# One attention-and-experts kernel on Trainium2: one SBUF tile for all buffers, or a tile for each

## The chip, the cores and the metric

The kernel runs on one core of one Trainium2 chip. The metric is the device time of one execution in microseconds (us); the medians below are over several executions. The engines are TensorE (PE; its weight loads are listed as PEld), VectorE (DVE), ScalarE (ACT), GpSimd (POOL) and SyncE (SP), which here only issues transfers. Each engine runs its own list of instructions in order, and waits on semaphores for the others.

## The reference

Sparse attention over 8 batches, 8 heads, 576 positions and 64 features, then a mixture of 8 experts that takes at most 80 tokens each:

```python
scores = scale * np.matmul(q, k.transpose(0, 1, 3, 2))
mask_local = (rel >= 0) & (rel < stride)                       # stride 32, heads 0-3
mask_strided = (rel >= 0) & (pos[None, :] % stride == pos[:, None] % stride)   # heads 4-7
attn = softmax(np.where(masks, scores, -1e9))
x = (attn @ v)  ->  [4608, 512]
logits = x @ w_gate; expert_idx = argmax(logits)
for e in range(8):                # at most `capacity` tokens, those with the highest gates
    h = np.maximum(x[tok_idx] @ w1[e], 0.0)
    out[tok_idx] = gate_w[tok_idx, None] * (h @ w2[e])         # all other rows stay zero
```

## The kernel before

The **attention stage** works through eight batches in a software pipeline. For each batch SyncE loads `ql` and `kl` (the local heads), `qs` and `ks` (the strided heads) and the values `vl`, `va`, `vb`; q and k have two sets of buffers, which batches take in turn, and the values have one. TensorE computes the scores (L324 local, L399 strided, after mask matmuls as L320), ScalarE and VectorE the softmax (L337 to L358 local, L409 to L425 strided), VectorE transposes the weights in blocks of 32, GpSimd and ScalarE put these blocks where the second product wants them (the `c4` copies, L206 on ScalarE, L208 on GpSimd and VectorE), TensorE multiplies by the values (L378 local, L440 strided) and turns the results (L532, L537), and the rows of x go to DRAM (`xs`) through the buffers `xn` and `xr`. Gate logits are computed on the way.

The **expert stage** ranks the gates, gathers 80 rows for each expert, and multiplies by `w1` (L793) and `w2` (L821). The weights are 64 pieces of 0.52 MB, each loaded to one of 35 places in turn (`w0` to `w63`, L580) and most of them split by ScalarE and VectorE (steps `wh`, `wo`) into two half-precision pieces (L609, L611). Ten places are memory of their own; 13 lie over the q and k buffers, eight over the value and weight buffers of attention and four over `xn` and `xr`, and are taken once attention is done with these. The rows of `out` that no expert writes are filled by 18 transfers of zeros (`z0` to `z17`, L558), and the scatters (L852) write the experts' rows after them.

The **order** of the work is written out: a string `ORDER` names each step (`lk` loads kl, `sk` ks, `sq` qs, `va` and `vb` the strided values, `c4` the copies, `u` and `d` the expert products), and each engine gets its steps in that order. SyncE's list is thus fixed, with attention loads, weights, stores and zeros in one row. Waits are not written out. The tile framework derives them from the tiles and the pieces of tiles that an instruction reads and writes.

All buffers are pieces of one tile `mem` of 128 partitions by 50304 words; a class `Area` hands out column ranges. Four kinds of loads write every second or every 16th partition of their piece: `tkl[h][u::2, u, ...]` (kl, L304, and L929 ahead of the loop), `tks[h][x::2, x]` (ks, L310 and L932), `tvs[0::2]` (va, L314) and `tvs[1::16]` (vb, L315). There are 16 + 16 + 8 + 8 = 48 such transfers in the program.

Of the kernel before, what the change touches and what calls it, by code (L numbers as in the profile page):

```python
# [86 lines left out]
def moe_attention(ctx: ExitStack, tc, ql, kl, qs, ks, vl, va, vb, wg, w1, w2, cap, out):  # L87
# [60 lines left out]
    a = Area(QK)
    tql, tkl, tqs, tks = [], [], [], []
    for i in range(2):  # L150
        tql.append(a([2, S]))
        tkl.append(a([2, 2, 32 + S]))
        tqs.append(a([4, 16, 18]))
        tks.append(a([2, 4, 16, 18]))
    assert a.at == PV
    tvl, ptb, tvs, pts4 = a([2, 9, D]), a([9, 2, 160]), a([32, D]), a([32, 4, 18])
    assert a.at == CB
    pl, ptl = a([2, 9, 64]), a([2, 9, 2, 32])
    pstr = [a([32, 18]) for _ in range(2)]
    psn, pts = a([32, 32]), a([32, 32])  # L160
    assert a.at == XT
    xtl = [a([2, S]) for _ in range(2)]
    xts = [a([4, S // 2]) for _ in range(2)]
    assert a.at == ROW
    xn = [a([2, DM]) for _ in range(3)]
    xr = a([2, DM])
    assert a.at == MISC
    lt, zt = a([S // 2]), a([1024])
    small = [[a([32]) for _ in range(4)] for _ in range(2)]
    gsm = [a([18, E], parts=NQ) for _ in range(2)]  # L170
    gs1 = [a([18], parts=NQ) for _ in range(3)]
    lgs = a([48, E], parts=NQ)
    assert a.at <= SPARE
    spare = [mem[:, SPARE + 512 * i:SPARE + 512 * i + 512] for i in range(2)]
# [3 lines left out]
    a = Area(CB)  # L178
    rtb = Area(a.at)
    a.at += 1380  # L180
# [1 line left out]
    hes = [a([2, 8, SLOTS], F16) for _ in range(2)]
# [1 line left out]
    assert a.at <= XT
    a = Area(XT)
# [1 line left out]
    assert a.at <= ROW
# [376 lines left out]
    def raw(i):  # L564
        return mem[:, bases[i % NSLOT]:bases[i % NSLOT] + CH]

    def hi(i):
# [3 lines left out]
        at = bases[split[s - 2] % NSLOT]  # L571
        return mem[:, at + 512:at + CH].bitcast(F16)
# [458 lines left out]
sl1.2 vb.1 es0.0/A c4l3.0/G sq.4 sml.1 c4s1.1/A c4s3.1/G w2 lk1.3 pvl0.0/0 c4s2.1/A lk0.3 sal.1/V wh0 pvl2.0/2 srl.1
lq.3 mx1.2 nl1.1 wgl0 pvl1.0/1 el0.0/A mxs.2 lk0.4 el2.0/A nl0.1 sbs.2 rs0.0/0 el1.0/A lv.1 rs1.0/2 c4s0.1/A lk1.4
ws0.0/V rl2.0/1 sk0.4 exs.2 trl.1 ss0.3 w3 ws1.0/A sk1.4 pvs1.1/0 wl2.0/A sb1.2 c4l5.1/G pvs2.1/2 es1.1/A c4l7.1/G
sms.2 pvs0.1/1 wh1 tk mx0.2 ss1.3 es0.1/A sb0.2 c4l3.1/G rl0.0/0 es2.1/A tk1/1 c4l6.1/G ex0.2 rs0.1/2 rc1 wo0 ex1.2
ss2.3 ws0.1/A sl0.3 sml.2 c4l4.1/G c4l1.1/A sas.2/G c4l2.1/G wl0.0/A ss3.3 sal.2/V c4l0.1/A srl.2 srs.2 rl1.0/2 nl1.2
# [90 lines left out]
```

## Time and profile before

| | |
|---|---|
| time, three runs | 442.89, 443.5, 445.39 us (median 443.5) |
| the profiled execution's own time | 439.65 us |
| its span in the trace | 437.9 us, 10778 instructions |
| mean granted TensorE clock | 0.767 of full speed |
| PE / PEld / DVE / ACT / POOL busy | 245.8 / 201.8 / 198.4 / 169.4 / 106.1 us |
| busy shares | 56% / 46% / 45% / 39% / 24% |
| DMA | 84.14 MB, mean 192 GB/s |
| chain that ended last | DMA 45%, PE 19%, issue 16%, POOL 7%, DVE 6% |

The profile was taken from one execution. "Busy" is the time in which an engine carried out an instruction; the chain is followed back from the last instruction to what released each step. [...] Attention takes the span up to about 333 us, the experts the rest; the two stages have different limits, so the shares over the whole span describe neither.

### The profile page before, as it was taken

To read this page: it belongs to the slowest core of one execution; us is meant where nothing else is said; L and a number is where in the kernel's file an instruction comes from. 1 tells how busy PE (TensorE), PEld (TensorE's weight loads), DVE (VectorE), ACT (ScalarE), POOL (GpSimd) and SP (SyncE) were. 2 spreads that over 40 slices of the span, in tenths; PEclk is the share of its full clock that TensorE was granted. 3 is DMA by queue.
4 is the path that set the end of the run, shared out by engine and by line. 5 is a ranking of instruction groups with operands and counts; after the bars stand their busy time and mean duration, and the time that the engine had idled before them with its cause. 6 is when DMAs were issued, how large, how long until landed. Compare 5 with 4: busy or idle time off the path is not lost.

```text
span 437.9 us, 10778 instructions
## 1 busy us (share of the span) xinstructions
PE 245.8 (56%) x4628; PEld 201.8 (46%) x4628; DVE 198.4 (45%) x326; ACT 169.4 (39%) x265; POOL 106.1 (24%) x158
## 2 busy tenths in 40 slices
PE   2426153414805446064706438657586798879894
PEld 2314042303703345044505325536475787779872
DVE  2312543101614244061233136625397759878871
ACT  3302141201703423132223234445366348778770
POOL 4300341110800323060213123336402420111101
PEclk9955685655776679557576659888698899998998
DMA  4444632443137265323314445775398999999701
GB/s 138 159 135 163 220 147 79 158 139 103 62 108 270 80 217 153 121 82 114 111 54 172 146 158 153 296 262 190 146 381 306 374 305 411 414 395 409 302 18 34
DMA packets 24613, 84.14 MB, mean 192 GB/s; under 512 B 4273, under 2 KB 4273, under 8 KB 23986
## 3 DMA queue, kind: packets, MB, share of 16 engines
q1 hardware_dynamic: 23538, 80.79, 52.1%
q0 software_dynamic: 1024, 2.62, 1.9%
q8 instruction: 38, 0.62, 0.6%
q14 instruction: 13, 0.11, 0.1%
HBM read 63.21 MB, written 20.19 MB: 190 GB/s over the span
## 4 chain that ended last, share of the span: by engine, by line
DMA 45%; PE 19%; issue 16%; POOL 7%; DVE 6%; SPq 3%; ACT 2%; POOLq 0%; DVEq 0%; ACTq 0%
DMA mem<-kl 10%; DMA mem<-ks 7%; DMA mem<-va 7%; DMA mem<-vb 5%; DMA mem<-w 4%; DMA mem<-ql 4%; DMA xs<-mem 3%; PE bk L532 3%; POOL mem L208 3%; PE bk L378 2%; DMA mem<-xs,mem 2%; DMA mem<-qs 2%; POOL out L852 2%; PE bk L537 2%; PE bk L793 2%
## 5 line engine op out<-in xcount | busy, mean ns | idle before, releaser
L611 DVE SCALAR_TENSOR_TENSOR mem<-mem 128x1024 f16<-128x1024 f32 x60 | 72.3, 1238 | 20.8 <-DMA mem<-kl 16.1
L206 ACT COPY mem<-bk 128x512 f32<-128x512 f32 (+4 forms) x85 | 44.3, 539 | 96.3 <-DMA mem<-ks 30.8
L208 POOL COPY mem<-mem 32x576 f32<-32x576 f32 (+1 forms) x65 | 44.8, 690 | 137.4 <-DMA mem<-ks 61.2
L609 ACT ACTIVATE mem<-mem 128x1024 f16<-128x1024 f32 x60 | 62.0, 1053 | 12.5 <-DVE mem L611 8.6
L532 PE MATMUL bk<-ident,mem 128*128 128x128 f32 (+1 forms) x96 | 20.4, 355 | 56.7 <-DMA mem<-kl 21.1
L206 ACT COPY mem<-mem 32x576 f32<-32x576 f32 (+1 forms) x31 | 20.7, 668 | 57.6 <-DMA mem<-ks 21.2
L532 PEld LDWEIGHTS bk<-ident,mem 128*128 128x128 f32 (+1 forms) x96 | 14.0, 183 | 61.0 <-issue 41.2
L324 PE MATMUL sloc<-mem 128*32 128x128 f32 x576 | 26.4, 342 | 16.5 <-DMA mem<-ks 16.5
L324 PEld LDWEIGHTS sloc<-mem 128*32 128x32 f32 x576 | 20.1, 138 | 28.7 <-issue 28.1
L793 PEld LDWEIGHTS <-mem 128*128 128x128 f16 x768 | 30.4, 100 | 5.0 <-issue 4.9
L378 PE MATMUL bk<-mem 128*64 128x160 f32 (+2 forms) x352 | 28.5, 325 | 6.9 <-ACT mem L206 5.2
L821 PE MATMUL sstr<-mem 128*128 128x80 f16 x672 | 30.8, 205 | 2.7 <-issue 2.6
L378 PEld LDWEIGHTS bk<-mem 128*64 128x64 f32 x352 | 26.3, 166 | 9.4 <-issue 4.6
L537 PE MATMUL bk<-ident,mem 128*128 128x128 f32 (+1 forms) x96 | 18.7, 333 | 20.8 <-ACT mem L206 20.8
L821 PEld LDWEIGHTS <-mem 128*128 128x128 f16 x672 | 27.7, 102 | 4.6 <-issue 4.4
L399 PEld LDWEIGHTS sstr<-mem 128*18 128x18 f32 x1024 | 15.8, 124 | 27.7 <-issue 22.7
L440 PE MATMUL bk<-mem 128*64 128x72 f32 x512 | 23.5, 260 | 7.0 <-ACT mem L206 6.8
L852 POOL DMA_INDIRECT out<-mem x8 | 8.9, 1108 | 69.6 <-ACT mem L847 34.3
L440 PEld LDWEIGHTS bk<-mem 128*64 128x64 f32 x512 | 21.8, 166 | 8.3 <-ACT mem L206 7.2
L356 POOL TENSOR_TENSOR mem<-mem 128x576 f32<-128x576 f32 x16 | 18.2, 1152 | 29.5 <-DMA mem<-kl 20.0
L200 PE MATMUL sstr<-identb 128*128 128x128 bf16 x237 | 18.7, 254 | 10.3 <-DVE mem L676 4.0
L411 DVE TENSOR_TENSOR mem<-sstr,mem 128x576 f32<-128x576 f32 x8 | 6.1, 758 | 39.5 <-DMA mem<-va 16.8
(166 smaller groups left out, 376.9 us busy)
## 6 DMA issues: line engine op xcount, KB each, us to landing
mem<-w SPq DMA_DIRECT2D x64, 512.0 KB, 9.9
out<-mem SPq DMA_DIRECT2D x18, 512.0 KB, 7.1
xs<-mem SPq DMA_DIRECT2D x16, 512.0 KB, 3.4
mem<-ql SPq DMA_DIRECT2D x8, 576.0 KB, 3.8
mem<-kl SPq DMA_DIRECT2D x16, 288.0 KB, 3.0
mem<-qs SPq DMA_DIRECT2D x8, 576.0 KB, 4.7
mem<-ks SPq DMA_DIRECT2D x16, 288.0 KB, 3.0
mem<-vl SPq DMA_DIRECT2D x8, 576.0 KB, 6.3
```

The costliest lines, as they stand in the source:

```text
L200: nc.tensor.matmul(sstr[:, 896:1024], identb, identb, start=True, stop=True)
L206: nc.scalar.copy(o, i)
L208: eng[e].tensor_copy(o, i)
L324: nc.tensor.matmul(sloc[32 * g:32 * g + 32, 128 * c:128 * c + 128], tql[h][:, hh, 32 * t:32 * t + 32], tkl[h][:, :, hh, 32 * t:32 * t + 64 ...
L378: nc.tensor.matmul(t[64 * u:64 * u + 64, n0:n0 + z - a], tvl[:, u, c], ptb[:, c, u, a:z], start=(c == 3 * k), stop=(c == 3 * k - 1), tile_ ...
L440: nc.tensor.matmul(t[64 * x:64 * x + 64, c:c + 72], tvs[:, r], pts4[:, 2 * (r % 16) + r // 16].rearrange("p h j -> p (h j)"), start=True, ...
L532: nc.tensor.transpose(t[0:n, x, c], xv[:, c, x, 128 * a:128 * a + n], ident)
L537: nc.tensor.transpose(t[0:n, g], xh[:, g, 128 * a:128 * a + n], ident)
L609: op("wh%d" % i, {"ACT": 1.05}, lambda e: nc.scalar.activation(hi(i), raw(i), AF.Copy, scale=SC), [st["w%d" % i]] + prev, filler=True)
L611: op("wo%d" % i, {"DVE": 1.24}, lambda e: nc.vector.scalar_tensor_tensor(lo(i), raw(i), SC, hi(i), op0=ALU.mult, op1=ALU.subtract), [st["w ...
L793: nc.tensor.matmul(o[:, f], w[:, n:n + P], x[:, a, c], start=(c == 0 and i == 0 and f == 0), stop=(c == 3 and i == 2), skip_group_check=True)
L821: nc.tensor.matmul(o, w[:, n:n + P], x[:, b, 2 * c + a], start=(c == 0 and a == 0 and f == 0 and i == 0), stop=(c == 3 and a == 1 and i == ...
```

## The change

Every buffer becomes a tile of its own (`buf` below), one for each set where a buffer has two. The places for weights are pieces of 1024 columns inside these tiles. A place may no longer cross from one buffer into the next, so 33 places remain: ten of their own, 12 over q and k, seven over the values and copied weights and four over `xn` and `xr`. The expert stage's smaller buffers (`xes`, `hes`, `y32`, the ranking's `rt`, the gathered rows `xg`) are cut out of tiles of attention in the same way. The number of instructions on each engine stays as it was: 5061 on TensorE, 188 on SyncE, 267 on ScalarE, 318 on VectorE and 177 on GpSimd in the built programs.

```diff
-    mem = wctx.enter_context(tc.tile_pool(name="mem", bufs=1)).tile([P, MEM], F32, name="mem")
+    mem = wctx.enter_context(tc.tile_pool(name="mem", bufs=1))
+
+    def buf(name, shape, n=1, parts=P):
+        return [mem.tile([parts] + shape, F32, name=f"{name}{i}") for i in range(n)]
...
+    tql, tkl = buf("ql", [2, S], 2), buf("kl", [2, 2, 32 + S], 2)
+    tqs, tks = buf("qs", [4, 16, 18], 2), buf("ks", [2, 4, 16, 18], 2)
+    (tvl,), (ptb,), (tvs,), (pts4,) = buf("vl", [2, 9, D]), buf("ptb", [9, 2, 160]), buf("vs", [32, D]), buf("pts4", [32, 4, 18])
...
+    def places(t, m):
+        f = flat(t) if len(t.shape) > 2 else t
+        return [f[:, CH * j:CH * j + CH] for j in range(m)]
+
+    slots = buf("slot", [CH], NFREE)
+    for i in range(2):
+        slots += places(tkl[i], 2) + places(tql[i], 1) + places(tks[i], 2) + places(tqs[i], 1)
+    slots += places(ptb, 2) + places(tvs, 2) + places(pts4, 2) + places(tvl, 1)
+    for t in (*xn, xr):
+        slots += places(t, 1)
+    NSLOT = len(slots)
...
-            t = mem[0:parts, self.at:self.at + w]
-            self.at += w
+            x = next(x for x in self.tiles if x[1] + w <= x[0].shape[1])
+            t = x[0][0:parts, x[1]:x[1] + w]
+            x[1] += w
...
-    a = Area(QK)
-    tql, tkl, tqs, tks = [], [], [], []
-    for i in range(2):
-        tql.append(a([2, S]))
-        tkl.append(a([2, 2, 32 + S]))
...
-    bases = [FREE + CH * i for i in range(NFREE)] + [QK + CH * i for i in range(13)] + \
-            [PV + CH * i for i in range(8)] + [ROW + CH * i for i in range(4)]
-    NSLOT = len(bases)
...
     def raw(i):
-        return mem[:, bases[i % NSLOT]:bases[i % NSLOT] + CH]
+        return slots[i % NSLOT]
...
         if k < 6:
             return after(6, "sl1", "ss3")
-        if k < 13:
-            return after(6, "sl1", "ss3") + after(7, "sl1", "ss3")
-        if k < 21:
+        if k < 12:
+            return after(7, "sl1", "ss3")
+        if k < 19:
             return after(7, *["pv%s%d" % (x, j) for x in "ls" for j in range(3)])
-        return [[stores[12], stores[15]], [stores[13]], [stores[14]], after(4, "st2") + after(5, "st2") + after(6, "st2") + after(7, "st2")][k - 21]
+        return [[stores[12], stores[15]], [stores[13]], [stores[14]], after(4, "st2") + after(5, "st2") + after(6, "st2") + after(7, "st2")][k - 19]
...
-    rt = rtb
+    rt = Area(pl, *pstr)
```

In `ORDER` a few loads of the first four batches move by a step or two, and of the zeros z10 to z17 stand among later weights. The loops themselves are the same.

**SyncE, batch 1 of attention.** The rows are transfers in the order in which SyncE issues them, with the semaphores that each waits for where it isn't yet sure of them: `DMAHW` with a number is one of eight that count landed transfers, the others are engines. Before:

```order
L310 DMA mem_89<-ks 64x1152 [waits DMAHW5_49,DMAHW6_49,DVE_49,DMAHW7_49,Activation_49,Pool_49]
L310 DMA mem_89<-ks 64x1152 [waits DVE_49,Activation_49]
L315 DMA mem_89<-vb 8x2048 [waits DMAHW4_49,DMAHW3_49,Pool_49]
L308 DMA mem_89<-qs 128x1152 [waits DMAHW5_49,DMAHW1_49,PE_49]
L580 DMA mem_89<-w1 128x1024
L304 DMA mem_89<-kl 64x2x576 [waits DVE_49,DMAHW6_49,Activation_49,Pool_49]
L304 DMA mem_89<-kl 64x2x576 [waits Activation_49]
L307 DMA mem_89<-ql 128x1152 [waits DMAHW2_49,DMAHW1_49,DMAHW0_49]
```

After:

```order
L299 DMA ks1_96<-ks 64x1152 [waits DMAHW3_49]
L299 DMA ks1_96<-ks 64x1152 [waits DMAHW4_49]
L304 DMA vs0_99<-vb 8x2048 [waits DMAHW5_49]
L297 DMA qs0_93<-qs 128x1152 [waits DMAHW6_49,PE_49]
L568 DMA slot2_135<-w1 128x1024 [waits DMAHW7_49]
L293 DMA kl1_92<-kl 64x2x576 [waits DMAHW0_49]
L293 DMA kl1_92<-kl 64x2x576 [waits DMAHW1_49]
L296 DMA ql1_90<-ql 128x1152 [waits DMAHW2_49]
```

The transfers and their order are the same. The loads of ks, kl and vb waited for VectorE, ScalarE or GpSimd and for several transfers; each now waits for one landed transfer.

**GpSimd, the copies of batch 0 (L208 before, L201 after).** They read the transposed weights `ptl` or `pts` and write `ptb` or `pts4`. Before:

```order
L422 TENSOR_TENSOR mem_89<-mem_89 128x512 [waits DVE_49,Pool_49]
L422 TENSOR_TENSOR mem_89<-mem_89 128x64
L208 COPY mem_89<-mem_89 32x18x32 [waits DMAHW1_49,Pool_49]
L208 COPY mem_89<-mem_89 32x18x32
L208 COPY mem_89<-mem_89 32x16x32 [waits DMAHW4_49,DMAHW3_49]
L208 COPY mem_89<-mem_89 32x18x32 [waits DMAHW5_49]
L208 COPY mem_89<-mem_89 32x32x18 [waits DVE_49,PE_49]
L356 TENSOR_TENSOR mem_89<-mem_89 128x576 [waits DMAHW0_49,DVE_49,DMAHW1_49,Activation_49,Pool_49]
L356 TENSOR_TENSOR mem_89<-mem_89 128x576 [waits DMAHW4_49]
```

After:

```order
L411 TENSOR_TENSOR psn0_103<-ps1_106,sm13_124 128x512 [waits DVE_49,Pool_49]
L411 TENSOR_TENSOR psn0_103<-ps1_106,sm13_124 128x64
L201 COPY ptb0_98<-ptl0_102 32x18x32 [waits Pool_49]
L201 COPY ptb0_98<-ptl0_102 32x18x32
L201 COPY ptb0_98<-ptl0_102 32x16x32
L201 COPY ptb0_98<-ptl0_102 32x18x32
L201 COPY pts40_100<-pts0_104 32x32x18 [waits DVE_49,PE_49]
L345 TENSOR_TENSOR pl0_101<-pl0_101,sm11_122 128x576 [waits DVE_49,Activation_49,Pool_49]
L345 TENSOR_TENSOR pl0_101<-pl0_101,sm11_122 128x576
```

The copies and the products around them waited for landed transfers; now they wait for engines alone.

**SyncE, early in the expert stage: the first pieces of weights past the last place.** Before, where the 36th piece (w35) is the row with PE in its waits:

```order
L580 DMA mem_89<-w2 128x1024 [waits DMAHW1_49]
L580 DMA mem_89<-w2 128x1024 [waits DMAHW2_49]
L580 DMA mem_89<-w2 128x1024 [waits DMAHW3_49]
L558 DMA out<-mem_89 128x1024 [waits DMAHW4_49]
L558 DMA out<-mem_89 128x1024 [waits DMAHW5_49]
L580 DMA mem_89<-w2 128x1024 [waits DMAHW6_49,PE_49]
```

After, where the 34th (w33) and 35th (w34) are the rows with PE, and two of the zeros follow:

```order
L568 DMA xr0_114<-w2 128x1024 [waits DMAHW1_49]
L568 DMA slot0_133<-w2 128x1024 [waits DMAHW2_49,PE_49]
L568 DMA slot1_134<-w2 128x1024 [waits DMAHW3_49,PE_49]
L547 DMA out<-zt0_116 128x1024 [waits DMAHW4_49]
L547 DMA out<-zt0_116 128x1024 [waits DMAHW5_49]
```

Two pieces of weights that had places of their own now go to places whose last readers are TensorE's products with the third and the fourth piece of expert 0's w1 (steps u20.0 to u31.0), and two zeros stand behind them.

## Rows read from the trace of the kernel before

**Rows 1.** Windows: us from:to, length, busy time by engine, granted clock, DMA share, GB/s.

```profile
core 0: us, PE busy (x) PEld busy (x) DVE busy (x) ACT busy (x) POOL busy (x), PEclk, DMA share, GB/s
0.00:333.00 333.00, 161.93 (x2888) 124.85 (x2889) 124.64 (x222) 102.77 (x170) 87.75 (x140) 0.71 0.47 160
333.00:438.00 105.00, 83.84 (x1740) 76.91 (x1739) 73.75 (x104) 66.67 (x96) 18.32 (x19) 0.94 0.79 295
```

**Rows 2.** Chain of waits that ended last within 0 to 333 us, by line.

```profile
by line: DMA mem<-kl 13.1%; DMA mem<-ks 9.4%; DMA mem<-va 8.8%; issue 7.3%; DMA mem<-vb 6.6%; DMA mem<-ql 5.1%; DMA xs<-mem 4.2%; PE bk L532 3.7%; POOL mem L208 3.7%; DMA mem<-w 3.5%; PE bk L378 3.2%; DMA mem<-qs 2.7%; PE bk L537 2.2%; PE s
```

**Rows 3.** Waits of engines: who <- what: us in total, times, longest us.

```profile
POOL mem L208 <- DMA mem<-ks: 61.2, 6, 16.7
ACT mem L206 <- DMA mem<-ks: 52.0, 6, 13.9
```

**Rows 4.** Timeline: start us, us, engine line op, [idle before <-releaser], batch 1.

```profile
64.39 4.31 SPq L310 DMA_DIRECT2D mem<-ks  x2
71.28 0.61 POOL L208 COPY mem<-mem 32x512 f32<-32x512 f32 x1 [6.91 <-DMA mem<-ks]
71.30 2.36 PE L324 MATMUL sloc<-mem 128*32 128x128 f32 x40 [9.19 <-DMA mem<-ks]
71.92 0.61 SPq L315 DMA_DIRECT2D mem<-vb  x1
```

**Rows 5.** The page's DMA issues: times, KB each, us from issue to landing.

```profile
mem<-kl SPq DMA_DIRECT2D x16, 288.0 KB, 3.0
```

**Rows 6.** Waits of SyncE's queue.

```profile
SPq L314 <- PE bk L440: 15.7, 3, 7.5
```

**Rows 7.** Timeline of the start, SyncE and TensorE.

```profile
4.64 1.30 SPq L929 DMA_DIRECT2D mem<-kl  x2
8.71 0.34 SPq L930 DMA_DIRECT2D mem<-qs  x1
14.34 0.68 PE L399 MATMUL sstr<-mem 128*18 128x36 f32 x32 [7.19 <-DMA mem<-ks]
```

**Rows 8.** Windows, TensorE's columns alone, of L324, L440 and L399 by pairs.

```profile
22.60:42.80 20.20, 4.81 (x84) 0.50 0.47 142
264.90:281.80 16.90, 3.44 (x112) 1.00 0.74 258
84.00:114.50 30.50, 4.64 (x64) 0.50 0.34 104
264.90:281.80 16.90, 2.37 (x64) 1.00 0.74 258
84.00:114.50 30.50, 1.37 (x64) 0.50 0.34 104
264.90:281.80 16.90, 0.92 (x64) 1.00 0.74 258
```

**Rows 9.** Windows of two dense stretches, TensorE's columns alone.

```profile
264.90:281.80 16.90, 12.66 (x311) 1.00 0.74 258
316.10:333.00 16.90, 14.17 (x189) 1.00 0.90 345
```

**Rows 10.** Window in the expert stage, all columns.

```profile
390.00:410.00 20.00, 18.00 (x423) 17.54 (x421) 15.85 (x19) 15.50 (x22) 3.03 (x2) 0.91 1.03 408
```

**Rows 11.** Timeline of SyncE's queue in the expert stage.

```profile
344.94 4.78 SPq L580 DMA_DIRECT2D mem<-w  x4
351.24 2.68 SPq L558 DMA_DIRECT2D out<-mem  x2
```

**Rows 12.** Timeline of both engines, group in 0 to 333 us, the page's group.

```profile
151.50 2.88 DVE L611 SCALAR_TENSOR_TENSOR mem<-mem 128x1024 f16<-128x1024 f32 x2
151.76 1.53 POOL L208 COPY mem<-mem 32x576 f32<-32x576 f32 x1
L611 DVE SCALAR_TENSOR_TENSOR mem<-mem 128x1024 f16<-128x1024 f32 x11 | 14.2, 1308 | 16.2 <-DMA mem<-kl 16.1
L208 POOL COPY mem<-mem 32x576 f32<-32x576 f32 (+1 forms) x65 | 44.8, 690 | 137.4 <-DMA mem<-ks 61.2
```

More of the change, by code (lines that the diff above doesn't have):

```diff
@@ L126, in moe_attention, with flat, __init__ @@
     wctx = ExitStack()
-    mem = wctx.enter_context(tc.tile_pool(name="mem", bufs=1)).tile([P, MEM], F32, name="mem")
+    mem = wctx.enter_context(tc.tile_pool(name="mem", bufs=1))
+    def buf(name, shape, n=1, parts=P):
+        return [mem.tile([parts] + shape, F32, name=f"{name}{i}") for i in range(n)]
+    def flat(t):
+        d = " ".join("abcdefg"[i] for i in range(len(t.shape) - 1))
+        return t.rearrange("p %s -> p (%s)" % (d, d))
+    tql, tkl = buf("ql", [2, S], 2), buf("kl", [2, 2, 32 + S], 2)
+    tqs, tks = buf("qs", [4, 16, 18], 2), buf("ks", [2, 4, 16, 18], 2)
+    (tvl,), (ptb,), (tvs,), (pts4,) = buf("vl", [2, 9, D]), buf("ptb", [9, 2, 160]), buf("vs", [32, D]), buf("pts4", [32, 4, 18])
+    (pl,), (ptl,), (psn,), (pts,) = buf("pl", [2, 9, 64]), buf("ptl", [2, 9, 2, 32]), buf("psn", [32, 32]), buf("pts", [32, 32])
+    pstr = buf("ps", [32, 18], 2)
+    xtl, xts = buf("xtl", [2, S], 2), buf("xts", [4, S // 2], 2)
+    xn, (xr,) = buf("xn", [2, DM], 3), buf("xr", [2, DM])
+    (lt,), (zt,) = buf("lt", [S // 2]), buf("zt", [1024])
+    small = [buf(f"sm{i}", [32], 4) for i in range(2)]
+    gsm, gs1, (lgs,) = buf("gsm", [18, E], 2, NQ), buf("gs", [18], 3, NQ), buf("lgs", [48, E], 1, NQ)
+    spare = buf("spare", [512], 2)
+    def places(t, m):
[8 more added lines that the diff above has]
+    NSLOT = len(slots)
     class Area:
-        def __init__(self, at):
-            self.at = at
+        def __init__(self, *tiles):
+            self.tiles = [[t if len(t.shape) == 2 else flat(t), 0] for t in tiles]
         def __call__(self, shape, dt=F32, parts=P):
@@ L146, in __call__ @@
             return t
[L148 to L180 removed]
+    a = Area(ptl, psn, pts)
+    hes = [a([2, 8, SLOTS], F16) for _ in range(2)]
     xes = [a([2, 4, SLOTS], F16) for _ in range(2)]
[L182 removed]
     y32 = [a([4, SLOTS]) for _ in range(2)]
[L184 to L185 removed]
+    a = Area(*xtl, *xts)
     xg = [a([DM], parts=SLOTS) for _ in range(E)]
[L187 removed]
     psum = wctx.enter_context(tc.tile_pool(name="psum", bufs=1, space=PSUM))
@@ L570, in hi @@
             return spare[s].bitcast(F16)
[L571 to L572 removed]
+        return raw(split[s - 2])[:, 512:CH].bitcast(F16)
     def lo(i):
@@ L1031 @@
[L1031 to L1035, printed above, removed]
@@ L1067 @@
-gg.7 r1 rl1.7/1 rl2.7/2 wl2.7/A r3 warm/8 r2 ws1.6/A st1.6 rs1.7/2 r4 wl1.7/A st2.7 r7 rs0.7/0 st2.6 ws1.7/A r5
-ws0.7/A st0.7 st1.7 w23 r6 w24 w25 w26 w27 wh11 warm/68 r8 z8 r13 r9 z9 wh12 z10 wo11 warm/14 r10 w28 w29 w30 r11 wh13
-r12 g0 w31 w32 wo12 w33 w34 z11 r14 g1 wh14 z12 wo13 wo14 wh15 warm/102 xt0 wo15 wh16 r15 xh0 g2 wh17 xl0 wo16 warm/21
-u00.0 xt1 u01.0 wo17 xh1 u11.0 wh18 u10.0 xl1 g3 u21.0 r16 wh19 u01.1 wo18 u20.0 u11.1 w35 wo19 wh20 u21.1 u00.1 xt2
-wo20 wh21 u30.0 u31.0 hh0.0 wo21 u10.1 xh2 w36 u20.1 wh22 w37 g4 hl0.0 z13 u30.1 xl2 w38 d00.0 wh23 wo22 xt3 z14 z15
@@ new lines @@
+pvl1.7/1 wh9 gd.6 el2.7/V rs2.6/0 el1.7/A w22 wo9 wh10 gt0.7/2 ws2.6/V rl0.7/1 wo10 lt.7 gt1.7/0 wl0.7/A rl0.6/2 ga.7
+rs2.7/1 gb.7 rl1.6/0 ge.7 wl1.6/A gc.7 wl0.6/A rs0.6/0 gd.7 ws2.7/V ws0.6/A gr.7/2 rs1.6/0 st0.6 gg.7 r1 rl1.7/1
+rl2.7/2 wl2.7/A r3 warm/8 r2 ws1.6/A st1.6 rs1.7/2 r4 wl1.7/A st2.7 r7 rs0.7/0 st2.6 ws1.7/A r5 ws0.7/A st0.7 st1.7
+w23 r6 w24 w25 w26 w27 wh11 warm/68 r8 z8 r13 r9 z9 wh12 z10 wo11 warm/14 r10 w28 r11 wh13 r12 g0 w29 wo12 w30 r14 g1
+wh14 wo13 w31 wo14 wh15 w32 warm/102 xt0 wo15 wh16 r15 xh0 g2 wh17 xl0 wo16 warm/21 u00.0 xt1 u01.0 wo17 xh1 u11.0
@@ new lines @@
+wh18 u10.0 xl1 g3 u21.0 r16 wh19 u01.1 wo18 u20.0 u11.1 w33 wo19 wh20 u21.1 u00.1 xt2 wo20 wh21 u30.0 u31.0 hh0.0 wo21
+u10.1 xh2 w34 u20.1 wh22 z11 g4 hl0.0 z12 u30.1 xl2 w35 d00.0 wh23 wo22 xt3 w36 w37 d10.0 hh1.0 u31.1 z13 hh0.1 wo23
+d01.0 wh24 w38 d11.0 g5 hl0.1 z14 wh25 u00.2 hl1.0 z15 wo24 d21.0 xh3 d20.0 z16 hh1.1 d31.0 xl3 g6 wh26 d30.0 hl1.1
+z17 u10.2 wo25 ya0/A u00.3 u01.2 w39 u20.2 wo26 wh27 u11.2 u01.3 w40 wo27 u21.2 wh28 d01.1 u31.2 w41 wo28 wh29 d00.1
+d11.1 u30.2 w42 wo29 wh30 d21.1 xt4 hh0.2 wo30 w43 yx0 wh31 u10.3 d10.1 hl0.2 w44 wh32 u11.3 wo31 u20.3 hh1.2 d20.1
```

99 lines of the change are left out of this document (45 added, 54 removed).

## The prediction

> **What bounds the kernel now.** I read the windows first, by stage [rows 1]. In the expert stage, the 105 us from 333 to 438, TensorE is busy for 83.84 us at a clock of 0.94 and the DMA engines move 295 GB/s: it is near its own limits. In attention, 0 to 333 us, nothing is: TensorE is busy for 161.93 us, VectorE 124.64, ScalarE 102.77, GpSimd 87.75, and DMA runs at 160 GB/s, where the expert stage shows stretches of 408 [rows 10]. So attention is bound by waits, and TensorE's clock is down to 0.71 meanwhile.
>
> Which waits, the chain of that stage tells [rows 2]: kl 13.1, ks 9.4, va 8.8 and vb 6.6%, together 37.9% of 333 us or 126 us, are landings of the four loads that write every second or 16th partition. Transfers of more bytes hold less of it: ql 5.1, qs 2.7, weights 3.5%. The waits by engine [rows 3] then name the oddity: the copies on GpSimd and ScalarE wait 61.2 and 52.0 us for loads of ks, six times each, up to 16.7 us. These copies read transposed softmax weights and never touch ks. The order of the built programs says the same: the strided loads wait for three compute engines, and the copies behind them for transfers.
>
> One place shows the whole pattern [rows 4]. From 64.39 SyncE holds two loads of ks. GpSimd's copy starts at 71.28, after 6.91 us idle, TensorE's scores of another buffer at 71.30 after 9.19, both released by ks; at 71.92 the load of vb closes the gate again. The cause is that a load that skips partitions is ordered against every access of its tile, and all buffers are one tile: the load waits until all engines have run dry, and all engines wait until it has landed. One landing takes 3.0 us [rows 5], so 48 loads have room for 144 us of landings, of which the chain holds 126.
>
> **The change part by part.** (1) *Tiles of their own* take these orderings away. In the built program a load waits for a transfer eight places back and for real readers of its own buffer, a copy for its producers. Real waits stay: va must wait until TensorE has read the values of the batch before (15.7 us, 3 times) [rows 6]. Instructions stay the same, so nothing is added.
>
> What is late next? Cover all with TensorE, the busiest engine. Its clock of 0.71 is a mix of 1.0 and 0.5; a share s at half gives 1 − 0.5s = 0.71, s = 0.58. If busy time is spread alike, 94 us of the 162 were done at half clock. What that costs is read from equal instructions at both levels [rows 8]: L324 takes 57.3 ns each at 0.50 and 30.7 at 1.00 (1.87), L440 72.5 and 37.0 (1.96), L399 21.4 and 14.4 (1.49); mean 1.77. At full clock the work is thus 94/1.77 + 68 = 121 us. TensorE won't be busy without a gap: in the two densest stretches of attention, both at clock 1.0, it is busy for 12.66 and 14.17 of 16.90 us [rows 9], shares of 0.75 and 0.84, mean 0.795. I take that, since those stretches have the same instructions and few strided loads in them: 121/0.795 = 152 us.
>
> Ahead of this stands the start. The first scores come at 14.34 [rows 7]; the loads of kl are issued at 4.64, after ql has landed, those of qs and ks from 8.71, after kl has. Both waits go, about 5 us by SyncE's rows, which leaves 9. Attention: 152 + 9 = **161 us instead of 333**. A second way, from the chain: 333 − 126 = 207, and less the 7.8% of ql and qs (26 us), which wait in the same row, 181 with the clock as slow as now. The faster clock explains the rest.
>
> DMA has to follow: 333 us at 160 GB/s are 53.3 MB; in 161 us that is 331 GB/s, just below the 345 of the densest stretch [rows 9], with no more than 131 us at 408 [rows 10]. So it fits, closely, and the other engines, with 125, 103 and 88 us of work, fit too.
>
> (2) *33 places instead of 35.* The pieces w33 and w34, and the zeros z11 and z12 behind them, now stand behind TensorE's products of expert 0. Before, SyncE issued pieces of weights and then zeros from 344.94 on, without waiting for TensorE, and the next zeros at 351.24 [rows 11]. A piece of 0.524 MB takes 1.28 us at 408 GB/s [rows 10], so four transfers held back cost at most 5.1 us, if the queue stays full afterwards, and nothing if it catches up. I take 0, because w33 belongs to w2 of expert 3, with the products of the experts ahead of it still to come, and keep 5.1 for the range. (3) *Zeros later, loads moved by a step*: the same bytes in another order on SyncE, hidden under TensorE; their cover is the 105 us at 295 GB/s, 31 MB that need 76 us at 408. 0.
>
> (4) *More overlap of VectorE and GpSimd* may cost. Where VectorE ran two of the weight splits (L611, 2.88 us from 151.50), one copy on GpSimd took 1.53 us in place of 0.69 on average [rows 12]. [...] By the row, 11 splits [rows 12] times 0.84 us are 9 us, if all fell on the path. They need not: GpSimd is free for 73 us of 161. I take 0 and keep 9.
>
> Sum: 161 + 105 = 266 us of span. The profiled execution took 439.65 with a span of 437.9, so 1.75 more: 267.8. The median of the runs, 443.5, is 1.0088 times that execution: **270 us**.
>
> **Its own bounds.** Below: at a busy share of 0.90, as in the expert stage (18.00 of 20 us) [rows 10], attention is 121/0.90 + 9 = 143, which gives 252; I say 250. Above: a share of 0.75 (161 us) and a quarter of the work still at half clock (0.25 × 0.77 × 161 = 31), with 9 for the start and 5 for the places, give 206 + 105 + 1.75 = 313, 315 scaled. Not all of this comes at once; without the places and with half of the clock's part it is 295. I say 305.
>
> **The rivals.** *The clock stays low.* If gaps remain often enough that it is granted 0.71 as before, 162/0.795 + 9 = 213 and the time is 322. For it: whole stretches stood at 0.50, as late as 114.5 us [rows 8]. Against: the gaps there are the removed waits. *Transfers become the bound.* At the 258 GB/s of the first dense stretch [rows 9] 53.3 MB take 207 us, and with the start the time is 326. For it: at most eight transfers are in flight, in one row, and a real wait of va holds all behind it. Against: 345 and 408 GB/s with the same queue. *VectorE and GpSimd run in turns.* 124.64 + 87.75 = 212 us [rows 1], with the start 221, time 331. Against: of 65 copies the mean is 0.69 [rows 12], so few are held. *The change does half of what it says*: enough waits remain, or copies really wait for something that lands with ks; attention (333 + 161)/2 = 247, time 357.
>
> *Slower.* If the waits for ks merely stood last beside real ones that end just as late, attention keeps its 333 us, and the loss of two places decides: 5.1 us more in the expert stage, 444.8 or 449 scaled (1.2%). It takes over only where attention gains less than 5.1 us. For it: a releaser is the last of several. Against: idle times of 6.91 and 9.19 us on two engines that end within 0.02 us of each other [rows 4], and a built order in which the copy has no other wait of that kind left.
>
> **How the numbers follow.** The forecast's case (250 to 305) has 0.80; the clock 0.05, transfers 0.04, turns 0.03, half 0.02, below 250 0.02, no change that can be told 0.02, slower 0.02. About 0.5% is what a measurement of this kernel can tell from no change. Faster is 0.80 + 0.05 + 0.04 + 0.03 + 0.02 + 0.02 = 0.96. The range is the forecast's own, which leaves out 0.20.
>
> **What would show it.** Right: no wait of a copy for kl, ks, va or vb among the first waits; attention ending near 161 us with a clock of 0.9 or more and over 300 GB/s; the first scores near 9 us; the expert stage still near 105. Wrong: the clock still near 0.7 there; SyncE's waits for real readers as the chain's largest part; copies on GpSimd of over 1 us in numbers; a gap in the weights after w32 with TensorE waiting for them.

## The result and the profile after

The changed kernel takes 277.19 us (median of four runs, 274.56 to 279.69) against 444.01 for the kernel before: a ratio of 0.6187, 95% interval 0.6154 to 0.622. The four runs lie in two pairs, near 274.7 and 279.6 us; here and below, medians are over all runs, while ratios and intervals leave out a run more than 1.5% above the fastest of the same kernel. The profiled execution took 274.93 us with a span of 273.2 us and a mean granted clock of 0.947.

Windows by stage, after, with the columns of [rows 1]. The border is put, here and in every kernel below, 1.6 us after the start of the last matmuls that turn attention's results, as 333.0 is in the kernel before.

```profile
0.00:165.80 165.80, 128.78 (x2883) 104.36 (x2889) 127.01 (x223) 100.86 (x169) 86.95 (x140) 0.95 0.89 320
165.80:273.20 107.40, 84.34 (x1740) 77.04 (x1739) 73.80 (x104) 66.78 (x96) 19.00 (x19) 0.94 0.79 289
12.10:165.80 153.70, 125.64 (x2858) 101.75 (x2864) 117.78 (x210) 93.37 (x162) 78.56 (x116) 0.94 0.90 325
```

Attention fell from 333.0 to 165.8 us; the expert stage stayed, 105.0 to 107.4. TensorE's busy time in attention fell from 161.93 to 128.78 us with the same work, as the clock (TensorE's granted clock, here and below) went from 0.71 to 0.95, and DMA went from 160 to 320 GB/s. VectorE, ScalarE and GpSimd are busy as long as before, in half the time.

The chain of attention, after, by line, beside [rows 2]; and the longest waits of engines and one of SyncE's queue, beside [rows 3] and [rows 6]:

```profile
by line: PE sloc L313 13.0%; issue 11.9%; PE bk L367 9.2%; PE bk L429 6.9%; PE sstr L388 4.9%; DMA kl<-kl 4.7%; DMA vl<-vl 4.3%; DMA ks<-ks 4.1%; PE bk L521 3.1%; PE sloc L309 3.1%; PE bk L526 2.8%; DVE sm L326 2.2%; DVE pl L328 1.8%; PE bk
```

```profile
POOL out L839 <- DVE ptl L791: 29.8, 1, 29.8
...
POOL pl L345 <- DVE sm L343: 18.4, 5, 8.4
...
DVE sm L326 <- PE sloc L313: 15.3, 6, 5.3
```

```profile
SPq L303 <- PE bk L429: 16.4, 3, 7.1
```

Landings of kl, ks, va and vb were 37.9% of attention's chain. Now kl and ks are 4.7 and 4.1% of a chain half as long, and TensorE's own lines lead it. Among the longest waits no copy waits for a load any more; engines wait for each other's results. The real wait of va for TensorE is what it was, 16.4 us in 3 against 15.7.

The place of [rows 4] in the kernel after, with the same two loads of ks and the load of vb, and GpSimd and VectorE beside them:

```profile
33.98 2.71 POOL L201 COPY ptb<-ptl 32x576 f32<-32x576 f32 x4
...
35.38 1.25 SPq L299 DMA_DIRECT2D ks<-ks  x2
...
36.67 0.61 SPq L304 DMA_DIRECT2D vs<-vb  x1
...
37.28 1.23 DVE L414 STREAM_TRANSPOSE pts<-psn 128x1024 f32<-128x1024 f32 x1
```

SyncE issues both loads of ks in 1.25 us, where they held it for 4.31, and vb right behind them. GpSimd's four copies run on while ks is issued, with no idle time ahead of them.

### The profile page after: what moved, and what is told of

It is laid out like the page before. It is cut to its first block, busy times and chain, and to the rows that moved or that the text cites. A ratio compares the mean times of both kernels' runs of the same rounds, so it can differ in the third digit from the quotient of the medians.

```text
span 273.2 us, 10660 instructions
## 1 busy us (share of the span) xinstructions
PE 213.1 (78%) x4623; PEld 181.4 (66%) x4628; DVE 200.8 (73%) x326; ACT 167.6 (61%) x265; POOL 106.0 (39%) x158
## 3 DMA queue, kind: packets, MB, share of 16 engines
q0 software_dynamic: 1024, 2.62, 3.0%
## 4 chain that ended last, share of the span: by engine, by line
PE 37%; issue 24%; DMA 15%; DVE 13%; ACT 3%; POOL 3%; SPq 2%; POOLq 0%; DVEq 0%; ACTq 0%
PE sloc L313 8%; PE sstr L193 6%; PE bk L367 6%; PE bk L429 4%; DMA out<-zt 4%; PE sstr L388 3%; DMA kl<-kl 3%; POOL out L839 3%; DMA slot<-w 3%; DMA vl<-vl 3%; DMA ks<-ks 2%; PE bk L521 2%; PE sloc L309 2%; PE bk L526 2%; DVE sm L326 1%
## 5 line engine op out<-in xcount | busy, mean ns | idle before, releaser
L201 POOL COPY ptb<-ptl 32x576 f32<-32x576 f32 (+1 forms) x47 | 32.9, 700 | 13.7 <-DVE ptl L347 7.4
L193 PE MATMUL sstr<-identb 128*128 128x128 bf16 x237 | 19.2, 254 | 12.6 <-DVE ps L663 3.9
L367 PE MATMUL bk<-ptb,vl 128*64 128x160 f32 (+2 forms) x352 | 24.0, 290 | 5.1 <-DVE g L508 3.2
L313 PE MATMUL sloc<-kl,ql 128*32 128x128 f32 x576 | 23.6, 307 | 5.4 <-issue 2.9
L388 PE MATMUL sstr<-ks,qs 128*18 128x36 f32 x1024 | 16.4, 205 | 13.9 <-issue 8.9
L345 POOL TENSOR_TENSOR pl<-pl,sm 128x576 f32<-128x576 f32 x16 | 18.1, 1155 | 23.2 <-DVE sm L343 18.4
L193 PEld LDWEIGHTS <-identb 128*128 128x128 bf16 x237 | 18.1, 117 | 13.4 <-issue 9.7
L367 PEld LDWEIGHTS bk<-ptb,vl 128*64 128x64 f32 x352 | 22.5, 144 | 6.2 <-issue 5.6
L199 ACT COPY xn<-bk 128x512 f32<-128x512 f32 x31 | 17.4, 580 | 12.8 <-PE bk L526 4.6
L326 DVE TENSOR_REDUCE sm<-sloc 128x8 f32<-128x512 f32 (+1 forms) x16 | 11.9, 746 | 15.3 <-PE sloc L313 15.3
L429 PE MATMUL bk<-pts,vs 128*64 128x72 f32 x512 | 18.6, 228 | 1.8 <-issue 1.2
L599 DVE SCALAR_TENSOR_TENSOR slot<-slot,slot 128x1024 f16<-128x1024 f32 x16 | 19.3, 1232 | 0.4 <-ACT slot L597 0.4
L429 PEld LDWEIGHTS bk<-pts,vs 128*64 128x64 f32 x512 | 17.3, 137 | 2.5 <-issue 2.3
L201 POOL COPY pts<-pts 32x576 f32<-32x576 f32 x18 | 12.0, 667 | 10.0 <-DVE pts L414 7.5
```

Of the source, the lines that this page charges most:

```text
L193: nc.tensor.matmul(sstr[:, 896:1024], identb, identb, start=True, stop=True)
L199: nc.scalar.copy(o, i)
L201: eng[e].tensor_copy(o, i)
L313: nc.tensor.matmul(sloc[32 * g:32 * g + 32, 128 * c:128 * c + 128], tql[h][:, hh, 32 * t:32 * t + 32], tkl[h][:, :, hh, 32 * t:32 * t + 64 ...
L326: op("mx%d.%d" % (i, b), {"DVE": 0.14 + n * 64 * 0.00105}, lambda e, sv=sv, mv=mv: nc.vector.tensor_reduce(mv, sv, op=ALU.max, axis=AX.X), ...
L345: op("nl%d.%d" % (u, b), {"POOL": 1.34}, lambda e, u=u: nc.gpsimd.tensor_tensor(pl[:, u], pl[:, u], sm[:, 9 * u:9 * u + 9].unsqueeze(2).br ...
```

## Experiments

Each kernel was timed beside the kernel before on the same chip, four kernels to a chip; medians of before there were 446.59, 446.69 and 444.49 us.

### Which property of the loads makes the waits

The first four kernels keep the order, the places and the zeros of the kernel after and put buffers back into one tile: all of them, all but kl, ks and vs, or all but vs.

```diff
+    OWN = ()    # one_tile; three_own: ("kl", "ks", "vs"); only_vs_own: ("vs",)
     def buf(name, shape, n=1, parts=P):
-        return [mem.tile([parts] + shape, F32, name=f"{name}{i}") for i in range(n)]
+        if name in OWN:
+            return [mem.tile([parts] + shape, F32, name=f"{name}{i}") for i in range(n)]
...
+            t = one[0:parts, used[0]:used[0] + w]
+            used[0] += w
```

> The kernel after with its own order of steps, its 33 places and its zeros, but all buffers again pieces of one tile. Theory (the waits come from one tile that holds all buffers, the order brings nothing): 435 to 455 us, attention ending near 333, the copies on GpSimd and ScalarE waiting 100 us and more for kl, ks, va and vb, the clock near 0.77. Rival (the moved loads and zeros carry a good part of the gain): under 400 us.

one_tile took 498.68 us, 1.1147 times the kernel before (1.1063 to 1.1232). The first theory's direction holds: with one tile the gain is gone, although the new order, the places and the zeros are kept. Its size is wrong: it had the time near the kernel before, and the run is 52 us above it, to which a later run returns.

> As the kernel after, but only kl, ks and vs are tiles of their own; all other buffers are pieces of one tile. Theory (only loads that skip partitions put a whole tile in order): 272 to 285 us, as the kernel after. Rival (any load into a shared tile orders it, so that ql, qs, vl, the weights and the stores' buffers take over): over 300 us.

three_own took 279.03 us (276.05 to 284.32), which these runs can't tell from the kernel after (274.56 to 279.69). Three kinds of buffers carry the gain; the others, among them ql, qs, vl, the ten free places and the stores' buffers, may share one tile at no cost that the runs can tell.

> Only vs is a tile of its own; kl and ks lie in the shared tile and skip partitions as before. Theory (each load that skips partitions is a barrier of its own, and va and vb held 15.4% of the chain in attention's 333 us, 51 us): about 392 us or somewhat more, since 32 of 48 barriers remain. Rival (barriers replace each other, so that removing a third gives nothing): over 430 us.

only_vs_own took 433.0 us, 0.9679 of before (0.9605 to 0.9753). Against one_tile, which differs from it in vs alone, that is 66 us for the 16 loads of va and vb; the 32 loads of kl and ks, taken away between only_vs_own and three_own, are worth the other 154. The chain of one_tile's attention stage (387.8 us), and then that of only_vs_own (323.9 us):

```profile
by line: DMA one<-kl 12.1%; DMA one<-ks 11.9%; DMA one<-w 9.7%; DMA one<-va 7.7%; DMA one<-ql 6.3%; PE sloc L332 5.5%; DMA one<-vb 5.0%; PE bk L386 4.7%; DMA xs<-one 3.5%; DMA one<-qs 2.9%; PE sstr L407 2.6%; issue 2.5%; PE bk L448 2.4%; PE
```

```profile
by line: DMA one<-kl 14.7%; DMA one<-ks 14.5%; DMA one<-ql 7.2%; DMA one<-w 7.2%; PE sloc L332 6.6%; PE bk L386 5.6%; DMA one<-vl 3.8%; DMA one<-qs 3.6%; DMA out<-one 3.3%; DMA xs<-one 3.2%; issue 3.1%; PE bk L448 2.8%; PE sloc L328 1.9%; P
```

The rival's number came, over 430 us, and the theory's 392 did not, but the rival's reason does not follow. Both had counted from the kernel before, and the arrangement that only_vs_own shares with one_tile costs 52 us by itself. Against one_tile, 16 of the 48 loads are worth 66 of the 220 us between one_tile and three_own, and va and vb held 12.7% of one_tile's chain, 49 us. The loads that are left hold what they held, 24.0% of 387.8 us and 29.2% of 323.9, 93 and 95 us: no sign that one barrier takes the place of another.

The fourth kernel tells the skipped partitions from the shared tile. It is only_vs_own with kl and ks written to 64 adjoining partitions; the rows of q are laid out to match.

```diff
-nc.sync.dma_start(tkl[h][u::2, u, :, 32:32 + S], kl[b, u])
+nc.sync.dma_start(tkl[h][64 * u:64 * u + 64, u, :, 32:32 + S], kl[b, u])
-nc.sync.dma_start(tks[h][x::2, x], ks[b, x])
+nc.sync.dma_start(tks[h][64 * x:64 * x + 64, x], ks[b, x])
```

> Only vs is a tile of its own; kl and ks lie in the shared tile, but their loads write 64 adjoining partitions, 64 u to 64 u + 63, in place of every second one, and the rows of q are laid out to match in DRAM, so the result is the same. Theory (it is the skipped partitions, not the shared tile): 272 to 290 us. Rival (the shared tile is enough): as only_vs_own, 390 us or more.

It took 294.04 us, a ratio of 0.6559 (0.6506 to 0.6612): 139 us off only_vs_own with the same tiles. That is the cause shown from the other side: with loads that write adjoining partitions, no wait of an engine for a load that it doesn't read is left among the longest, though the tile is shared; in only_vs_own GpSimd's copies wait 42.0 us for ks and 40.5 for kl. It is 15 us slower than three_own, above the theory's range too, and the transfers are the likely reason. Windows of the start, in which the first loads of k (64 partitions each) and of q (all 128) land, side_by_side and then three_own:

```profile
5.00:12.00 7.00, 1.68 (x14) 1.19 (x12) 6.32 (x8) 3.30 (x4) 5.00 (x11) 0.88 1.00 247
```

```profile
5.00:12.00 7.00, 1.90 (x27) 1.37 (x29) 6.32 (x8) 3.30 (x4) 5.00 (x11) 1.00 0.94 306
```

With the DMA engines busy for all of the time, adjoining partitions bring 247 GB/s; every second partition brings 306 at a share of 0.94. Over all of attention, side_by_side and then three_own:

```profile
0.00:185.90 185.90, 133.46 (x2888) 106.45 (x2889) 126.91 (x223) 101.86 (x169) 88.61 (x140) 0.90 0.94 286
```

```profile
0.00:167.40 167.40, 128.74 (x2888) 104.27 (x2889) 127.69 (x223) 101.98 (x170) 86.80 (x140) 0.95 0.89 317
```

The share is higher, 0.94 against 0.89, and the rate lower, 286 GB/s against 317: the same bytes hold the engines longer, 175 us of full DMA time in attention (0.94 x 185.9) against 149 (0.89 x 167.4). Why the engines move less with k written so, no run shows. TensorE also has the lower clock, 0.90 against 0.95, and more unexplained idle time in the chain ("issue", 31 us against 20), so that the 15 us are not shown to be the transfers' alone. The tiles are the faster remedy of the two.

### The 52 us that one tile costs more than the kernel before

one_tile_old_order is one_tile with the string `ORDER` of the kernel before, where w33 and later pieces wait in it until their place is free:

```diff
-ss0.1 vb.0 fpsn/A sb1.0 lk1.2 ss1.1 sms.0 ex1.0 ss2.1 lk0.2 sas.0/V srs.0 sml.0 ss3.1 lq.2 ns1.0 ns0.0 sl0.1 w0
+ss0.1 vb.0 fpsn/A sb1.0 lk1.2 ss1.1 lk0.2 sms.0 ex1.0 lq.2 ss2.1 sas.0/V w0 srs.0 sml.0 w1 ss3.1 ns1.0 ns0.0 lv.0
```

> All buffers pieces of one tile with 33 places, as one_tile, but the steps in the order of before (w33 and later pieces where their place is free). Theory (the 52 us by which one_tile was slower than before come from the new order of loads among the barriers): 440 to 452 us. Rival (they come from the 33 places or from where the buffers lie in the tile): about 490 us.

It took 499.27 us (two executions): the theory fell, the order is not it, and the rival's 490 came near. What differs from the kernel before is then the 33 places and where the buffers lie in the tile. The traces show one place where the time sits. Waits of TensorE's strided scores for loads, one_tile (L407) and then the kernel before (L399):

```profile
PE sstr L407 <- DMA one<-ks: 36.5, 5, 9.5
...
PE sstr L407 <- DMA one<-va: 16.3, 2, 10.1
...
PE sstr L407 <- DMA one<-vb: 14.6, 2, 11.3
...
PE sstr L407 <- DMA one<-kl: 13.3, 3, 6.8
```

```profile
PE sstr L399 <- DMA mem<-ks: 7.2, 1, 7.2
```

In the kernel before these scores waited for one load, their first, for 7.2 us; in one_tile these four make 80.7 us, and 44.2 of them are for va, vb and kl, which the scores don't read. In the built programs the second step of batch 0's strided scores waits for the load of batch 1's ks in the new arrangement and not in the old. So in the kernel before some accesses escaped the ordering. That their columns in the tile decide it fits, but no run changed the columns alone, and the rule by which they escape stays open.

### Order, zeros and places

Three kernels change the order of SyncE's transfers alone, and after_again is the kernel after beside them.

> The kernel after, unchanged, so that the three runs beside it have their measure on the same chip. 274 to 280 us.

It took 278.54 us, 0.6239 of before (0.621 to 0.6269).

old_order is the kernel after with that same order of before. zeros_in_gap puts z11 to z17 ahead of w33, zeros_early puts z10 to z17 in pairs ahead of va of batches 3 to 6:

```diff
-u01.1 wo18 u20.0 u11.1 w33 wo19
+u01.1 wo18 u20.0 u11.1 z11 z12 z13 z14 z15 z16 z17 w33 wo19
...
-z1 c4l1.3/A c4l4.3/G sb0.4 va.3
+z1 c4l1.3/A c4l4.3/G sb0.4 z10 z11 va.3
```

> The kernel after with the steps in the order of before: zeros z10 to z17 and the loads of batches 0 to 3 at their old positions; pieces of weights from w33 on come later where their place is not free yet. Theory (with tiles of their own the order of loads and zeros is worth little): within 1% of the kernel after, on either side. Rival (the later zeros pay for the two lost places): slower by 5 us or more, all of it in the expert stage.

277.17 us, 0.6221 (0.6194 to 0.6248), and an expert stage of 106.1 us: no difference that the runs can tell. The new order of loads and zeros is worth nothing here, as predicted.

> The kernel after with z11 to z17 ahead of w33, where SyncE waits 12 us for TensorE (181 to 193.5 us of its trace). Theory (transfers bound the expert stage from there on, and the queue runs thin at 196 to 198 us, 238 GB/s): 1 to 4 us faster, the transfers ending 1 to 4 us earlier. Rival (the queue of eight covers the wait, or TensorE bounds the stage): no change, or slower by weights that land later.

276.67 us, 0.6201 (0.6175 to 0.6227): the intervals overlap, and the expert stage of its trace is 107.6 us long, as in after_again. SyncE's wait at w33 costs nothing that the runs can tell. Transfers already issued cover it: in the kernel after the DMA engines are busy throughout the wait.

```profile
181.00:193.50 12.50, 10.09 (x186) 9.60 (x185) 4.97 (x8) 4.54 (x6) 4.54 (x5) 0.93 1.03 330
```

In zeros_in_gap the transfers thin out earlier (72 GB/s from 246 to 253 us, where the kernel after has 246 GB/s from 245 to 252) and the stage still gains nothing, so they don't bound its end.

> The kernel after with z10 to z17 in attention, two ahead of each of va of batches 3 to 6, where SyncE waits for TensorE. Theory (the expert stage is bound by its 82 us of transfers, and attention has slack for 8 x 1.28 = 10 us of them): the expert stage 5 to 10 us shorter, attention 0 to 5 us longer, 268 to 275 us. Rival (attention, with its DMA engines busy for 0.89 of the time, is as full): attention longer by as much as the expert stage gains, 273 to 280.

276.49 us, a ratio of 0.6142 (0.6103 to 0.6181). That is below after_again's, but its interval overlaps that of the first measurement of the kernel after (0.6154 to 0.622), and its six runs, 272.89 to 280.81 us, overlap both: a gain is not shown. Its windows by stage:

```profile
0.00:167.80 167.80, 128.22 (x2888) 104.24 (x2889) 127.90 (x223) 101.42 (x171) 86.76 (x140) 0.96 0.94 342
167.80:272.40 104.60, 85.26 (x1740) 78.19 (x1739) 73.48 (x104) 66.04 (x95) 18.59 (x19) 0.93 0.71 256
```

Attention takes 4.2 MB more at 342 GB/s, with the DMA engines busy for 0.94, and ends at 167.8 us, between the two traces of the kernel after (165.8, and 168.6 in after_again). So attention had room for these transfers, as the theory said. The expert stage is 104.6 us, 3 shorter, not 5 to 10: transfers bound it for a part of its time at most. That TensorE's busy 85.26 us with the head before them hold the rest is the likely reading.

places_31 takes two of the ten places of their own away; where that leaves a piece without a free place, it comes later in the order.

```diff
-NFREE = 10
+NFREE = 8
```

> The kernel after with eight places of their own in place of ten, 31 in all; pieces of weights come later in the order where their place isn't free yet, among them w8, w9, w14, w15, w20 and w21 in attention and w31 to w38 after it. Theory (two places are worth nothing, since the expert stage is bound by TensorE and what feeds it, not by transfers): within 1% of the kernel after, the expert stage within 1 us. Rival (each pair of places costs the 2 to 3 us by which the expert stage grew): 2 to 5 us slower, in the expert stage.

274.32 us, 0.6181 (0.6143 to 0.6219), with an expert stage of 107.3 us against 107.4: two places fewer cost nothing that the runs can tell.

### The clock alone

clock_held is the kernel before with 12 matmuls that nothing reads (`warm`) ahead of 84 of TensorE's steps in attention, as here:

```diff
-mxs.1 nl1.0 sl1.1 sbs.1 nl0.0 trs.0 exs.1 ss0.2 mx0.1
+mxs.1 nl1.0 sl1.1 sbs.1 nl0.0 trs.0 exs.1 warm/12 ss0.2 mx0.1
```

> The kernel before with 84 groups of 12 matmuls that nothing reads, ahead of TensorE's steps in attention, so that TensorE is busy while it would wait; one tile as before. Theory (the waits set the time, and the slow clock is what they bring along): the clock above 0.85, the time 425 to 450 us. Rival (the clock carries a large part of the gain): under 400 us.

472.22 us, 1.0659 times before (1.0569 to 1.0749; two executions). Attention's window and the wait that [rows 3] has with 61.2 us:

```profile
0.00:368.10 368.10, 223.87 (x3910) 187.31 (x3911) 129.09 (x237) 104.79 (x175) 88.58 (x142) 0.77 0.43 146
```

```profile
POOL mem L208 <- DMA mem<-ks: 68.2, 6, 18.4
```

The clock in attention rose from 0.71 to 0.77 only, and attention grew to 368.1 us. Neither theory's numbers came. The run shows that filling the waits doesn't remove them; what the clock by itself is worth it does not tell, since the added matmuls stand on the path themselves.

### The start and the head of the expert stage

The kernel after has two places where its trace shows time that no work needs. At its start, first SyncE and TensorE, beside [rows 7], then the piece of the chain between them:

```profile
4.72 1.13 SPq L919 DMA_DIRECT2D ks<-ks  x2
```

```profile
12.11 0.69 PE L388 MATMUL sstr<-ks,qs 128*18 128x36 f32 x32 [4.96 <-DMA ks<-ks]
```

```profile
5.25 6.72 DMA ks<-ks
```

In the kernel before the chain had the same two loads with a shorter landing:

```profile
9.64 4.56 DMA mem<-ks
```

The loads of ks are issued 4.4 us earlier than before, but take 6.72 us to land, beside the loads of kl and of q that are then under way, where they took 4.56. The second place is the head of the expert stage. TensorE in the kernel after, from 178 us, and in the kernel before at the same step; L193 and L200 are the matmuls that only keep it busy, L765 and L778 turn the first expert's gathered rows:

```profile
178.26 6.53 PE L193 MATMUL sstr<-identb 128*128 128x128 bf16 x85 [2.37 <-DVE pl L706]
185.19 0.40 PE L193 MATMUL sstr<-identb 128*128 128x128 bf16 x4 [0.39 <-issue]
186.61 0.44 PE L193 MATMUL sstr<-identb 128*128 128x128 bf16 x5 [1.03 <-issue]
188.04 0.61 PE L193 MATMUL sstr<-identb 128*128 128x128 bf16 x8 [0.99 <-issue]
188.48 0.45 PE L765 MATMUL bk<-ident,xtl 80*128 80x80 f32 x4
```

```profile
345.56 7.48 PE L200 MATMUL sstr<-identb 128*128 128x128 bf16 x102 [2.37 <-DVE mem L719]
353.90 0.47 PE L778 MATMUL bk<-ident,mem 80*128 80x80 f32 x4 [0.86 <-DMA mem<-xs,mem]
```

Before, 102 such matmuls ran through in 7.48 us, and the rows were turned when the gather landed. After, they come with gaps of 0.39, 1.03 and 0.99 us that the profile puts down to nothing ("issue"), and the rows are turned when the matmuls are done. start_and_head is zeros_early with both edited; VectorE and ScalarE also change roles in clearing kl and ks, so that ks is clear first.

```diff
+    nc.sync.dma_start(tqs[0], qs[0])
     nc.sync.dma_start(tql[0], ql[0])
+    for x in range(2):
+        nc.sync.dma_start(tks[0][x::2, x], ks[0, x])
     for u in range(2):
         nc.sync.dma_start(tkl[0][u::2, u, :, 32:32 + S], kl[0, u])
-    nc.sync.dma_start(tqs[0], qs[0])
-    for x in range(2):
-        nc.sync.dma_start(tks[0][x::2, x], ks[0, x])
...
-warm/102 xt0
+warm/80 xt0
```

> zeros_early with two edits: ahead of the loop the loads of qs and ks come before those of kl, with VectorE clearing ks and ScalarE kl (the first scores need qs and ks alone), and the 102 matmuls that keep TensorE busy before the first expert are 80. Theory: first scores at 8 to 10 us instead of 12.1, of which 1 to 3 us are kept by the end of attention; the first expert's turned rows wait for the gather instead of for these matmuls, 1 to 2.4 us earlier; 270 to 275 us. Rival: the start is absorbed by later waits and the clock falls in the new gap: no change.

270.72 us (267.69 to 275.06), a ratio of 0.6051 (0.6 to 0.6102), below the interval of the kernel after: 2 to 3% faster than it, and the fastest of all. Its first scores, its first turned rows, and its stages:

```profile
7.85 0.46 PE L388 MATMUL sstr<-ks,qs 128*18 128x36 f32 x32 [0.93 <-DMA ks<-ks]
```

```profile
183.65 0.47 PE L765 MATMUL bk<-ident,xtl 80*128 80x80 f32 x4 [0.67 <-DMA xtl<-xs,pl]
```

```profile
0.00:164.40 164.40, 128.56 (x2888) 104.40 (x2889) 127.58 (x223) 101.65 (x171) 86.99 (x140) 0.95 0.94 349
164.40:266.90 102.50, 82.78 (x1718) 75.74 (x1717) 73.49 (x104) 66.40 (x95) 18.65 (x19) 0.94 0.72 261
```

The first scores come at 7.85 us, 4.3 earlier than in the kernel after and a little earlier than the theory's 8 to 10, and attention ends 3.4 us earlier than in zeros_early. The rows wait for the gather again, 19.3 us after the border instead of 22.7, more than the theory's 1 to 2.4, and the expert stage is 102.5 us. Which of the two edits brings how much of the time no run separates; the interval touches that of zeros_early (0.6103).

## Why the prediction was right, and what was off

The mechanism was right in the main. The time went from the waits for loads that skip partitions (three_own and side_by_side show both halves of that sentence), the clock rose with it (0.71 to 0.95), and nothing as long took the place of the waits. One step was too broad: that such a load is ordered against every access of its tile. In the kernel before some accesses escaped, as the strided scores show, and one_tile, where they don't, takes 52 us more. The forecast did not need that step, since it added up what remains and not what goes. The median came 7.2 us above the forecast, and so did the span, 273.2 against 266. Term by term:

| term | forecast | after |
|---|---|---|
| first scores | 9 us | 12.1 us |
| from there to attention's end | 152 us | 153.7 us |
| TensorE's work in attention; busy share from the first scores on | 121 us; 0.795 | 128.78 us at clock 0.95; 125.64/153.7 = 0.82 |
| DMA rate in attention | 331 GB/s | 320 GB/s |
| expert stage | 105 us | 107.4 us |
| outside the span; median to profiled run | 1.75 us; 1.0088 | 1.73 us; 1.0082 (luck: the median lies between two pairs of runs) |

- **The start** was mis-sized by 3.1 us. The step that took the waits' 5 us off the first scores counted when the loads are issued, and left their landing at its old length. The landing took 6.72 us in place of 4.56, which is 2.2 of the 3.1; the loads were issued 4.4 us earlier and not 5.3, which is the rest. In start_and_head, with the order of loads and of clearing changed, the first scores come at 7.85 us.
- **TensorE's term** was off by 1.7 us, the sum of two errors of opposite sign: nearly 5 us more busy time from the first scores on, as the clock stood at 0.94 there and not at 1.0, and a share of 0.82 where I took 0.795. That they cancel is luck.
- **The expert stage** grew by 2.4 us. I had kept up to 5.1 us for the two lost places; it is not they. places_31 has two fewer at no cost, zeros_in_gap fills the wait at no gain, and from the first product to the end the kernel after takes 83.1 us against 82.3, inside the 78.9 to 83.1 of these kernels. What grew most, by 1.9 us, is the way from the first gather (GpSimd's L735, L748 in the kernel before) to its rows being turned:

```profile
177.06 2.11 POOL L735 DMA_INDIRECT xtl<-xs,pl  x1 [10.53 <-DMA vs<-w]
```

```profile
344.34 2.13 POOL L748 DMA_INDIRECT mem<-xs,mem  x1 [10.60 <-DMA mem<-w]
```

| kernel | gather issued to rows turned | first product to end |
|---|---|---|
| before | 353.90 - 344.34 = 9.6 us | 82.3 us |
| after | 188.48 - 177.06 = 11.4 us | 83.1 us |
| clock_held (code of before) | 11.7 us | 81.3 us |
| places_31 | 11.5 us | 81.6 us |
| zeros_early | 11.9 us | 78.9 us |
| start_and_head | 8.1 us | 79.6 us |

The gaps among the matmuls of the head, 2.4 us in the kernel after, account for it, less the 0.86 us that the kernel before waited for its gather in the same stretch. They don't come from the change: clock_held, whose expert stage is the code of the kernel before, has 2.6 us of them (its idle time ahead of these matmuls, from 370 to 395 us).

```profile
  issue: 2.6, 3
```

The trace of the kernel before has none there and one of 1.23 us later, among its first products (362.78). start_and_head, with 80 matmuls in place of 102, has 1.4 us of them.

- **VectorE beside GpSimd** at 0 was right. The copies took 32.9 us for 47 and, in a second group of the page, 12.0 for 18: 691 ns each, and 690 in [rows 12], though VectorE and GpSimd were each busy for twice the share of attention (0.77 and 0.52 after, 0.37 and 0.26 before).

```profile
L201 POOL COPY ptb<-ptl 32x576 f32<-32x576 f32 (+1 forms) x47 | 32.9, 700 | 13.7 <-DVE ptl L347 7.4
...
L201 POOL COPY pts<-pts 32x576 f32<-32x576 f32 x18 | 12.0, 667 | 10.0 <-DVE pts L414 7.5
```

- **The rivals.** The clock did not stay low (0.95), transfers did not bind (zeros_early brought 342 GB/s through the same queue), and the engines did not take turns (VectorE and GpSimd were busy for 127 and 87 us within 165.8). The slower rival needed waits for ks that stand beside real ones; attention's fall by 167 us leaves no room for them. The rival of "half of what it says" fell with the measured time; what such a state looks like only_vs_own shows, 433.0 us with 32 of the 48 barriers left.

## What to carry to other kernels

When an engine is shown waiting for a load that it doesn't read, look at how that load writes its tile: here those that skip partitions ordered other engines' accesses to the rest of the tile, and giving their buffers tiles of their own was enough, 279.03 us against the 498.68 of one_tile; the rest could stay together. To cost the removal of such waits, take the busiest engine's work at the clock that it will then have over its busy share in the densest stretch, and add the start, with landings at the length that they have beside the loads then under way, for ks 6.72 us here and not 4.56. Here this came out to 1.7 us for TensorE's term by two errors that cancelled, and 3.1 us off at the start. SyncE's wait from 181 to 193.5 us was worth nothing that the runs can tell: issued transfers covered it, with 330 GB/s through it.
